# The opening of a sliding-window attention and feed-forward kernel, issued in another order

## Chip, cores, metric

One NeuronCore of one Trainium2 chip. The metric is the device time of one execution in microseconds (us); a median of several runs is given.

## What is computed

Attention over 8 batches, 8 heads, 576 positions and 64 features per head, in which a position sees only those at most 32 away, followed by a feed-forward pair with a leaky ReLU between:

```python
B, H, S, D = q.shape                       # 8, 8, 576, 64
scores = (q @ k.transpose(0, 1, 3, 2)) / sqrt(D)
scores = where(abs(pos[:, None] - pos[None, :]) <= 32, scores, -1e9)
attn = exp(scores - max(scores));  attn = attn / sum(attn)
x = (attn @ v).transpose(0, 2, 1, 3).reshape(B * S, H * D)      # 4608 x 512
h = x @ w_in                               # 512 x 2048
out = maximum(0.01 * h, h) @ w_out         # 2048 x 512, result 4608 x 512 f32
```

## The kernel before

The kernel's instructions go to each engine in the order in which the program writes them; nothing reorders them. So the order of the lines is the order of every engine's queue, and an engine whose next instruction waits holds all that is behind it.

The work is cut into units `i`: a unit is one batch, one half of the positions (288 queries) and one pair of heads. Eight units make a batch; units 0 to 3 are the first half of batch 0 for its four pairs, units 4 to 7 the second half. A unit goes through these steps:

- `score(i)` (L270): five matmuls on PE into the one score buffer `ps`, the exponential on ACT (L280, `e`), and the product with the band mask on POOL (L282, `prob`). The next unit's matmuls need the exponential to have read `ps`.
- `sums(i)` (L295): on PE the sum over keys of `prob`, by two matmuls with a block of ones into the one buffer `s` (L304), then the reciprocal on DVE (L309, `r`).
- `product(i)` (L312): five matmuls of `prob` with the values into the one buffer `x` (L320).
- `scaled(i)` (L332): `x` times `r` on DVE into `xT` (L334), the input of the feed-forward part; it frees `x`.

Ahead of a unit the queries, keys and values of its pair must be ready. `load_qk` and `load_v` load them in f32 by DMAs on SP's queue (`qf`, `kf`, `vf`). `cast_qk` (L186) casts to bf16: the queries on DVE or ACT, as its argument says, the keys on POOL. `transposes(0)` (L218) is a generator: each `next(first)` makes six PE transposes of a pair's queries, or then of its keys (L225), and their copy out of PSUM on ACT (L233, L239). `place_keys` (L248) copies transposed keys into the block-diagonal `kbd` on DVE, two copies a pair (L258). `cast_v` (L199) casts the two heads' values into the block-diagonal `vbd`, on POOL (L205) or ACT (L203). `make_mask` makes a half's band mask in two POOL copies (L163, L165).

`load_w_in` and `load_w_out` (L447, L450) load the weights, cast to bf16 on the way, in four DMAs each, issued on POOL's queue, where each issue takes its place among POOL's work. `keep_busy(t, lo, n)` (L398) is n matmuls without a use, in an unused part of `t`, that keep PE working (L402).

The feed-forward part goes by half batches: `h_first(0)` (L369) runs the first four tiles of h with the contraction outermost, so that each `next(h0)` needs one more pair's `xT`; `h_tile` (L360) then runs the others, 16 tiles for a half. From there on PE has dense work, into which the attention of later units is woven: `second_half()` (L525) inserts units 4 to 7 of batch 0 after chosen tiles, and from batch 1's second half on a plan with due times (L571 to L618) does so. `o_tile` (L382) is the second matrix product. The change touches only the opening, L461 to L505, up to the first `next(h0)`.

Of the kernel before, what the change touches and what calls it, by code (L numbers as in the profile page):

```python
# [16 lines left out]
def kernel(  # L17
# [14 lines left out]
    nc = tc.nc  # L32
# [128 lines left out]
    def make_mask(hf):  # L161
        lo = (16, 32)[hf]
        nc.gpsimd.tensor_copy(out=mask[hf][:, 0], in_=win_f[:, :, lo:lo + EVEN])  # L163
        lo = (16, 0)[hf]
        nc.gpsimd.tensor_copy(out=mask[hf][:, 1, :, lo:lo + 128], in_=win_f[:, :, 0:128])  # L165
# [4 lines left out]
    ps = scps.tile([128, 1024], FP32)  # L170
# [15 lines left out]
    def cast_qk(b, p, q_eng=None):  # L186
        for eng, src, dst in ((q_eng or nc.gpsimd, qf, qb), (nc.gpsimd, kf, kb)):
            if b < BY_DMA:
                parts = [(dst[:, p], src[b, p].rearrange("p a (c d) -> p c a d", d=D))]
            else:  # L190
                by_c = src[b, p].rearrange("p a (g c d) -> c p g a d", g=3, c=2)
                parts = [(dst[:, p, 3 * c:3 * c + 3], by_c[c]) for c in range(2)]
            for to, tok in parts:
                if eng is nc.scalar:
                    eng.activation(out=to, in_=tok, func=AF.Copy)
                else:
                    eng.tensor_copy(out=to, in_=tok)  # L197

    def cast_v(b, p, on_act=False):  # L199
        for a in range(2):  # L200
            r = slice(64 * a, 64 * a + 64)
            if on_act:
                nc.scalar.activation(out=vbd[b % 2][r, p, :, r], in_=vf[b, p][r], func=AF.Copy)  # L203
            else:
                nc.gpsimd.tensor_copy(out=vbd[b % 2][r, p, :, r], in_=vf[b, p][r])  # L205
# [42 lines left out]
    def place_keys():  # L248

        while landing and landing[0][0] <= state["done"]:  # L250
            unplaced.append(landing.pop(0)[1:])
        while unplaced:
            b, p, kT = unplaced.pop(0)
            for a in range(2):
                r = slice(64 * a, 64 * a + 64)
                to = kbd[b % 2][r, p, :, r]
                if b < BY_DMA:
                    nc.vector.tensor_copy(out=to, in_=kT[r].rearrange("p (n j) -> p n j", j=64))  # L258
                else:
                    nc.vector.tensor_copy(  # L260
                        out=to.rearrange("p n (m c) -> p n c m", c=2),
                        in_=kT[r].rearrange("p (c n m) -> p n c m", c=2, n=NB),
                    )
# [3 lines left out]
    def where(i):  # L267
        return i // 8, (i // 4) % 2, i % 4

    def score(i):  # L270
        b, hf, p = where(i)
        by_c = qT[b][:, p].rearrange("p (c i) -> p c i", c=2)
        for n_, blocks in enumerate(WIN[hf]):
            for blk, i0, n in blocks:
                nc.tensor.matmul(  # L275
                    ps_v[:, n_, :, i0:i0 + n], kbd[b % 2][:, p, blk],
                    by_c[:, :, hf * EVEN + i0:hf * EVEN + i0 + n], start=True, stop=True,
                )
        e = attn.tile([128, 2 * HALF], BF16, name="e")
        nc.scalar.activation(out=e, in_=ps[:, P0:P0 + 2 * HALF], func=AF.Exp, scale=scale)  # L280
        pr = prob[:, i % NPROB]
        nc.gpsimd.tensor_mul(  # L282
            pr.rearrange("p n c i -> p (n c i)"), e, mask[hf].rearrange("p n c i -> p (n c i)"),
        )
        probs[i] = [pr, None, None]
# [9 lines left out]
    def sums(i):  # L295

        b, hf, p = where(i)
        pr, both, _ = probs[i]
        s = xps.tile([128, HALF], FP32, name="s")
        if both is not None:  # L300
            nc.tensor.matmul(s, ones_bd, both, start=True, stop=True)  # L301
        else:
            for n in range(2):
                nc.tensor.matmul(  # L304
                    s, ones_bd, pr[:, n].rearrange("p c i -> p (c i)"),
                    start=(n == 0), stop=(n == 1),
                )
        r = recip.tile([128, HALF], FP32, name="r")
        nc.vector.reciprocal(r, s)  # L309
        probs[i][2] = r  # L310

    def product(i):  # L312

        b, hf, p = where(i)
        pr = probs[i][0]
        x = xps.tile([128, HALF], FP32, name="x")
        x_v = x.rearrange("p (c i) -> p c i", c=2)
        parts = [(n_, *block) for n_ in range(2) for block in WIN[hf][n_]]
        for n_, blk, i0, n in parts:
            nc.tensor.matmul(  # L320
                x_v[:, :, i0:i0 + n], vbd[b % 2][:, p, blk, :], pr[:, n_, :, i0:i0 + n],
                start=(blk == parts[0][1]), stop=(blk == parts[-1][1]), skip_group_check=True,
            )
        probs[i][1] = x

    def place(i):

        b, hf, p = where(i)
        t0 = (b * S + hf * HALF) % RING
        return xT[:, p, t0:t0 + HALF]  # L330

    def scaled(i):  # L332
        _, x, r = probs.pop(i)
        nc.vector.tensor_mul(place(i), x, r)  # L334
# [11 lines left out]
    def h_mms(g, f, h, cs):  # L346
        for c in cs:
            nc.tensor.matmul(  # L348
                h[:, 0:HALF], w_in_bf[:, c, ts(f, 128)], xT[:, c, ds(g * HALF % RING, HALF)],
                start=(c == 0), stop=(c == DMC - 1),  # L350
            )

    def h_out(g, f, h):

        nc.scalar.activation(  # L355
            out=gT[:, f, ds(g * HALF % RING, HALF)].rearrange("p (i c) -> p i c", c=2),
            in_=h[:, 0:HALF].rearrange("p (c i) -> p i c", c=2), func=AF.Prelu, alpha=0.01,
        )
# [10 lines left out]
    def h_first(g):  # L369

        hs = [mmps.tile([128, 512], FP32, name="mm", tag="mm") for _ in range(4)]
        yield hs[0]
        for c in range(DMC):
            for f in range(4):
                h_mms(g, f, hs[f], (c,))
            if c == DMC - 1:
                for f in range(4):
                    h_out(g, f, hs[f])
            yield
# [18 lines left out]
    def keep_busy(t, lo, n):  # L398


        for _ in range(n):
            nc.tensor.matmul(  # L402
                t[:, lo:lo + 224], ones_bd, mask[0].rearrange("p n c i -> p (n c i)")[:, 0:224], start=False, stop=False,
                skip_group_check=True,
            )
# [14 lines left out]
    def step():  # L420


        i = state["done"]
        if JOINED - 1 <= i < NC - 1:
            join(i + 1)
        if i < NC - 2:
            score(i + 2)
        weighted(i)
        place_keys()
        for b, p in qk_due.get(i, ()):  # L430
            cast_qk(b, p)
            transpose_dma(b, p)
            if 2 < b < B - 1:
                load_qk(b + 1, p)
        if 12 < i <= 12 + NPAIR:
            load_qk(3, i - 13)
        for b, p in v_due.get(i, ()):
            cast_v(b, p)
            if b + 1 < B:
                load_v(b + 1, p)  # L440
        state["done"] += 1
# [5 lines left out]
    def load_w_in(f0, f1):  # L447
        nc.gpsimd.dma_start(out=w_in_bf[:, :, f0:f1], in_=w_in_r[:, :, f0:f1])  # L448

    def load_w_out(i):  # L450
        c = slice(4 * i, 4 * i + 4)
        nc.gpsimd.dma_start(out=w_out_bf[:, c, :], in_=w_out_r[:, c, :])

    first = transposes(0)

    def first_pair():
        next(first)
        next(first)
        place_keys()
# [2 lines left out]
    make_mask(0)  # L462
    cast_qk(0, 1, nc.vector)
    first_pair()
    first_pair()
    cast_v(0, 0)
    score(0)
    cast_qk(0, 2, nc.vector)
    score(1)
    sums(0)  # L470
    next(first)
    next(first)
    product(0)
    keep_busy(ps, 0, 2)
    place_keys()
    cast_qk(0, 3, nc.scalar)
    load_w_in(0, 512)
    scaled(0)
    sums(1)
    keep_busy(ps, 0, 3)  # L480
    load_w_in(512, 1024)
    load_w_in(1024, 1536)
    next(first)
    score(2)
    next(first)
    cast_v(0, 1, on_act=True)
    load_w_in(1536, 2048)
    make_mask(1)
    place_keys()
    keep_busy(ps, 0, 8)  # L490
    sums(2)
    score(3)
    load_w_out(0)
    product(1)
    scaled(1)
    cast_v(0, 2, on_act=True)
    score(4)
    h0 = h_first(0)
    h = next(h0)
    keep_busy(h, HALF, 8)  # L500
    product(2)
    scaled(2)
    sums(3)
    cast_v(0, 3, on_act=True)
    load_w_out(1)  # L505

# [140 lines left out]
```

## Time and profile before

| | |
|---|---|
| median of 3 runs | 319.5 us (319.1 to 320.05) |
| profiled execution: span, first to last instruction | 318.5 us |
| around the span: median less span | 1.0 us |
| PE, DVE, ACT, POOL busy | 95%, 69%, 57%, 60% |
| TensorE clock granted | 1.000 from 19.15 us on |
| first dense matmul of h (third `next(h0)` complete) | 26.39 us |

Of the profiled execution the profile gives the span, and no other time of its own. A row of a group or of the timeline has a start in us from the span's start, a length, the engine, the line, the operation and the tiles it writes and reads (`out<-in`); "x5" is five instructions merged. PE stands for matmuls, PEld for weight loads. The chain is the sequence of work that ended last, followed backwards from the last instruction. The length of a matmul in a row is from its issue to its modelled end; the next can be issued well before that.

### The profile page before, as it was taken

The page shows a single profiled execution, that of the slowest core. Times are in us where ns is not written, and L with a number is a line of the kernel's source. Part 1 is how long each engine was busy: PE and PEld are TensorE (multiplying, and loading weights), DVE is VectorE, ACT ScalarE, POOL GpSimd, SP SyncE. Part 2 cuts the span into 40 slices and gives each one's busy share as a digit, 9 for nine tenths or more (in the row PEclk, how much of TensorE's full clock was granted, in tenths as well). Part 3 has the DMA queues.
Part 4 walks back from the last instruction along what each step waited for, and adds up shares of the span by engine and source line. Part 5 has one row for each costly group of instructions (what it writes and reads, how often), then busy time and mean ns, then how long its engine had stood idle before and what let it go on. Part 6 is the DMA issues. An engine that isn't in the chain of part 4 may idle for free.

```text
span 318.5 us, 6474 instructions
## 1 busy us (share of the span) xinstructions
PE 303.2 (95%) x2449; PEld 204.3 (64%) x2449; DVE 218.2 (69%) x259; ACT 182.6 (57%) x393; POOL 191.6 (60%) x251
## 2 busy tenths in 40 slices
PE   2679998999999999999999999999999999999996
PEld 1467774585765858576765858576665858576653
DVE  5678955869655997688755997688745988565100
ACT  7577698474652828374652828375552837464531
POOL 7798963974546866686546866586637866330000
PEclk9999999999999999999999999999999999999999
DMA  8999999997999995399735995399733430000101
GB/s 179 211 186 218 267 250 203 250 206 181 216 242 196 231 206 150 82 251 203 155 76 127 238 227 136 75 223 232 162 76 104 109 70 33 35 35 2 66 31 71
DMA packets 108400, 49.46 MB, mean 155 GB/s; under 512 B 68816, under 2 KB 103888, under 8 KB 108368
## 3 DMA queue, kind: packets, MB, share of 16 engines
q1 hardware_dynamic: 104144, 44.84, 66.8%
q0 software_dynamic: 4224, 4.19, 8.0%
q8 instruction: 19, 0.31, 0.4%
q14 instruction: 13, 0.11, 0.1%
HBM read 36.70 MB, written 9.44 MB: 145 GB/s over the span
## 4 chain that ended last, share of the span: by engine, by line
PE 89%; DMA 3%; DVE 2%; SPq 1%; POOL 1%; ACT 1%; issue 1%; DVEq 0%; ACTq 0%
PE mm L348 39%; PE mm L390 38%; PE x L320 5%; PE ps L275 4%; DMA kf<-in_k_dram 3%; PE s L301 2%; DVE r L309 2%; SPq L79 1%; POOL w_in_bf L448 1%; DVE xT L334 1%; PE tp L225 1%; PE s L304 1%; ACT vbd L203 0%; SPq L91 0%; POOL prob L282 0%
## 5 line engine op out<-in xcount | busy, mean ns | idle before, releaser
L309 DVE RECIPROCAL r<-s 128x288 f32<-128x288 f32 x64 | 125.2, 1956 | 56.5 <-PE s L301 53.3
L282 POOL TENSOR_TENSOR prob<-e,mask 128x576 bf16<-128x576 bf16 x64 | 81.5, 1274 | 87.8 <-ACT e L280 41.1
L348 PE MATMUL mm<-xT,w_in_bf 128*128 128x288 bf16 x1024 | 134.0, 286 | 0.3
L390 PE MATMUL mm<-w_out_bf,gT 128*128 128x512 bf16 (+2 forms) x592 | 130.4, 373 | 0.2 <-DMA w_out_bf<-in_moe_w_out_dram 0.2
L355 ACT ACTIVATE gT<-mm 128x288 bf16<-128x288 f32 x256 | 101.4, 412 | 24.8 <-PE mm L348 8.5
L348 PEld LDWEIGHTS <-w_in_bf 128*128 128x128 bf16 x1024 | 98.4, 98 | 24.8 <-issue 0.6
L390 PEld LDWEIGHTS <-gT 128*128 128x128 bf16 x592 | 56.3, 98 | 59.6 <-issue 0.3
L395 ACT ACTIVATE o_sb<-mm 128x512 f32<-128x512 f32 (+2 forms) x37 | 21.7, 586 | 92.0 <-PE mm L390 92.0
L280 ACT ACTIVATE e<-ps 128x576 bf16<-128x576 f32 x64 | 41.4, 648 | 9.4 <-PE ps L275 9.2
L197 POOL CAST kb<-kf 96x384 bf16<-96x384 f32 (+1 forms) x56 | 35.5, 656 | 4.6 <-DMA kf<-in_k_dram 4.6
L205 POOL CAST vbd<-vf 64x576 bf16<-64x576 f32 x50 | 34.5, 689 | 1.8 <-DMA vf<-in_v_dram 0.4
L334 DVE TENSOR_TENSOR xT<-x,r 128x288 bf16<-128x288 f32 x64 | 29.3, 458 | 8.2 <-PE x L320 1.2
L260 DVE COPY kbd<-kT 64x576 bf16<-64x576 bf16 x48 | 32.3, 672 | 0.3
L275 PE MATMUL ps<-qT,kbd 128*128 128x128 bf16 (+2 forms) x320 | 26.5, 215 | 1.8 <-DVE kbd L258 1.2
L275 PEld LDWEIGHTS <-kbd 128*128 128x128 bf16 x320 | 21.0, 100 | 10.6 <-DVE kbd L258 1.5
L320 PE MATMUL x<-prob,vbd 128*128 128x128 bf16 (+2 forms) x320 | 26.0, 213 | 1.3 <-ACT vbd L203 0.7
L197 POOL CAST qb<-qf 96x384 bf16<-96x384 f32 x48 | 24.5, 538 | 0.0
L320 PEld LDWEIGHTS <-vbd 128*128 128x128 bf16 x320 | 20.6, 99 | 3.9 <-ACT vbd L203 1.8
L292 DVE TENSOR_TENSOR both<-prob 128x288 bf16<-128x288 bf16 x52 | 19.7, 380 | 0.9
L301 PE MATMUL s<-both,ones_bd 128*128 128x288 bf16 x52 | 14.9, 286 | 0.0
L258 DVE COPY kbd<-kT 64x576 bf16<-64x576 bf16 x16 | 7.1, 444 | 8.7 <-ACT kT L239 8.6
L225 PE MATMUL tp<-ident,qb 96*128 96x96 bf16 x48 | 4.4, 243 | 6.2 <-DVE qb L197 6.2
(43 smaller groups left out, 86.6 us busy)
## 6 DMA issues: line engine op xcount, KB each, us to landing
qf<-in_q_dram SPq DMA_DIRECT2D x32, 288.0 KB, 4.5
kf<-in_k_dram SPq DMA_DIRECT2D x32, 288.0 KB, 5.0
vf<-in_v_dram SPq DMA_DIRECT2D x64, 144.0 KB, 4.2
out_dram<-o_sb SPq DMA_DIRECT2D x35, 256.0 KB, 3.6
w_in_bf<-in_moe_w_in_dram POOLq DMA_DIRECT2D x4, 512.0 KB, 8.6
w_out_bf<-in_moe_w_out_dram POOLq DMA_DIRECT2D x4, 512.0 KB, 16.8
qT<-qb SPq DMA_TRANSPOSE x24, 4.1
kT<-kb SPq DMA_TRANSPOSE x24, 3.2
```

What stands on the lines that cost most here:

```text
L197: eng.tensor_copy(out=to, in_=tok)
L205: nc.gpsimd.tensor_copy(out=vbd[b % 2][r, p, :, r], in_=vf[b, p][r])
L260: nc.vector.tensor_copy(out=to.rearrange("p n (m c) -> p n c m", c=2), in_=kT[r].rearrange("p (c n m) -> p n c m", c=2, n=NB),)
L275: nc.tensor.matmul(ps_v[:, n_, :, i0:i0 + n], kbd[b % 2][:, p, blk], by_c[:, :, hf * EVEN + i0:hf * EVEN + i0 + n], start=True, stop=True,)
L280: nc.scalar.activation(out=e, in_=ps[:, P0:P0 + 2 * HALF], func=AF.Exp, scale=scale)
L282: nc.gpsimd.tensor_mul(pr.rearrange("p n c i -> p (n c i)"), e, mask[hf].rearrange("p n c i -> p (n c i)"),)
L309: nc.vector.reciprocal(r, s)
L320: nc.tensor.matmul(x_v[:, :, i0:i0 + n], vbd[b % 2][:, p, blk, :], pr[:, n_, :, i0:i0 + n], start=(blk == parts[0][1]), stop=(blk == parts ...
L334: nc.vector.tensor_mul(place(i), x, r)
L348: nc.tensor.matmul(h[:, 0:HALF], w_in_bf[:, c, ts(f, 128)], xT[:, c, ds(g * HALF % RING, HALF)], start=(c == 0), stop=(c == DMC - 1),)
L355: nc.scalar.activation(out=gT[:, f, ds(g * HALF % RING, HALF)].rearrange("p (i c) -> p i c", c=2), in_=h[:, 0:HALF].rearrange("p (c i) -> ...
L390: nc.tensor.matmul(o[:, lo:hi], gT[:, f, ds(128 * j % RING, 128)], w_out_bf[:, f, lo:hi], start=(f == 0), stop=(f == FFC - 1),)
```

## The change

`cast_v` gets an argument that says which of the two heads to cast. In the opening, the first pair's scores are issued ahead of the second pair's key transposes, with the second half of the first value cast behind them; sums 0 (and so reciprocal 0) ahead of the cast of queries 2, which goes from DVE to ACT; score 2 ahead of query transposes 3; the weight DMAs one or two at a time between POOL's casts and mask products, in place of three ahead of the third mask product; the second mask behind the fourth mask product; and sums 3 (with its reciprocal) ahead of `scaled(2)`.

```diff
-    def cast_v(b, p, on_act=False):
-        for a in range(2):
+    def cast_v(b, p, on_act=False, heads=range(2)):
+        for a in heads:
             r = slice(64 * a, 64 * a + 64)
...
     make_mask(0)
     cast_qk(0, 1, nc.vector)
     first_pair()
-    first_pair()
-    cast_v(0, 0)
+    next(first)
+    cast_v(0, 0, heads=(0,))
     score(0)
-    cast_qk(0, 2, nc.vector)
+    cast_v(0, 0, heads=(1,))
+    next(first)
+    place_keys()
+    sums(0)
+    cast_qk(0, 2, nc.scalar)
     score(1)
-    sums(0)
+    product(0)
     next(first)
     next(first)
-    product(0)
+    scaled(0)
+    place_keys()
     keep_busy(ps, 0, 2)
-    place_keys()
-    cast_qk(0, 3, nc.scalar)
     load_w_in(0, 512)
-    scaled(0)
     sums(1)
     keep_busy(ps, 0, 3)
+    cast_qk(0, 3, nc.scalar)
     load_w_in(512, 1024)
-    load_w_in(1024, 1536)
-    next(first)
     score(2)
     next(first)
+    next(first)
+    keep_busy(ps, 0, 8)
     cast_v(0, 1, on_act=True)
+    load_w_in(1024, 1536)
     load_w_in(1536, 2048)
-    make_mask(1)
     place_keys()
-    keep_busy(ps, 0, 8)
     sums(2)
     score(3)
-    load_w_out(0)
+    make_mask(1)
     product(1)
     scaled(1)
     cast_v(0, 2, on_act=True)
     score(4)
+    load_w_out(0)
     h0 = h_first(0)
     h = next(h0)
     keep_busy(h, HALF, 8)
     product(2)
+    sums(3)
     scaled(2)
-    sums(3)
     cast_v(0, 3, on_act=True)
     load_w_out(1)
```

## The prediction

> **What bounds the kernel now.** I read the page first, then the chain that ended last from 0 to 45 us, then the timeline of the opening, the windows and PE's waits. The page:
>
> ```profile
> span 318.5 us, 6474 instructions
> PE 303.2 (95%) x2449; PEld 204.3 (64%) x2449; DVE 218.2 (69%) x259; ACT 182.6 (57%) x393; POOL 191.6 (60%) x251
> ```
>
> PE is the bound. The windows (length, then each engine's busy time and count) show where it isn't:
>
> ```profile
> 19.15:22.57 3.42, 2.49 (x31) 2.01 (x28) 2.74 (x4) 2.73 (x5) 3.39 (x5) 1.00 1.24 206
> 25.98:29.40 3.42, 3.28 (x36) 2.63 (x35) 3.08 (x4) 2.69 (x8) 2.56 (x3) 1.00 1.24 202
> 61.00:318.50 257.50, 254.40 (x2002) 169.51 (x2000) 174.32 (x205) 136.59 (x309) 143.49 (x190) 1.00 0.66 140
> ```
>
> From 26.39 on PE stops four times, for 1.20 us in all: 0.13 at 37.46, 0.22 at 48.84 (w_out), 0.71 at 51.06 (vbd), 0.14 at 60.47. The order there isn't touched. The stops at 51.06 and 60.47 follow from PE's own transposes and sums, and the wait for w_out lies in front of the 0.71, which would take it up. So the span moves by as much as the dense stream starts sooner or later, and the chain of the opening says what starts it (start, length, what):
>
> ```profile
> 15.54 0.82 POOL kb L197
> 16.36 2.35 POOL w_in_bf L448 x3
> 18.72 0.01 issue
> 18.73 1.30 POOL prob L282
> 20.03 0.04 issue
> 20.07 0.42 PE s L304 x2
> 20.49 0.03 issue
> 20.52 1.97 DVE r L309
> 22.49 0.02 issue
> 22.51 0.47 DVE xT L334
> ...
> 23.02 0.41 PE x L320 x5
> 23.43 0.02 issue
> 23.45 0.46 DVE xT L334
> 23.91 1.88 DVE r L309
> ...
> 26.39 0.65 PE mm L348 x4
> ```
>
> Three weight issues on POOL stand before the third mask product, then DVE's reciprocals follow one another: 3.92 us from the end of reciprocal 2 (22.48) to 26.39. The clock of PE shows in the timeline's keep_busy rows, 3 in 0.77 us and later 8 in 0.93:
>
> ```profile
> 15.92 0.77 PE L402 MATMUL ps<-mask,ones_bd 128*128 128x224 bf16 x3
> 21.75 0.93 PE L402 MATMUL mm<-mask,ones_bd 128*128 128x224 bf16 x8
> ```
>
> That is 0.187 us apiece before and 0.096 after; the trace has full clock granted from 19.15.
>
> **The change, walked queue by queue.** Durations are the trace's: six transposes 0.66 (the next PE group may start after 0.48), PSUM copy 0.65, kbd pair 0.91, score or product 0.65 at half clock and 0.40 at full, sums 0.64 and 0.41, exp 0.65, mask product 1.27, reciprocal 1.95, scaled 0.46, hand-over 0.04 to 0.09. The same walk over the old order meets the trace within 0.2 us at each step.
>
> First scores. kbd 0 is ready at 8.69, but PE stands behind the key transposes until POOL's cast at 9.37. Now score 0 runs at 8.75, exp at 9.44, mask product 0 at 10.18 to 11.45 (was 11.46 to 12.73). Key transposes 1 still start at 9.43; their copy on ACT lands behind exp 0 at 10.12, where it was: no cost. The second half of the value cast slips to 11.41 to 12.08 on POOL, which is idle until kf 2 lands at 12.68, so it is hidden with 0.6 us; product 0, its only reader, starts at 12.4.
>
> Sums 0 at 11.51 (was 12.78), reciprocal 0 at 12.2 (was 13.45). Score 1 now waits behind sums 0: 11.95 (was 11.77). ACT's cast of q 2 (0.83, row of q 3) at 11.45 holds nothing. Both are hidden by mask product 1, which stands behind POOL's cast k 2, whose data land at 12.68 in either order. That cast took 1.09 beside DVE's f32 cast of 1.39, and 0.82 (k 3) beside other DVE work; DVE now does a reciprocal there, so I take 0.82 and keep 1.09 as the other end. It gives 13.55, key copy 2 at 14.31, kbd 2 at 15.00 to 15.91 (was 16.18).
>
> Weights. POOL's order was product 1, k 3, w_in x3, product 2; now product 1 (to 14.80), w_in 0 (0.93, to 15.69), k 3 to 16.47 (0.10 later), w_in 1 to 17.2, product 2. Score 2 no longer stands behind query transposes 3: 15.96 (was 16.97), exp 2 16.66 to 17.31 (was 17.75), mask product 2 17.40 to 18.67 (was 18.73 to 20.02). The eight keep_busy wait for exp 2 and take PE from 17.37 to 18.87, so sums 2 starts at 18.87 (was 20.07), and reciprocal 2 at 19.46: 1.06 us earlier.
>
> SP's queue keeps its order. w_in 0 issued 1.55 us earlier meets the last value loads; vf 3 landed at 19.05 and 19.74 and is read at 22.6 and 23.3, and product 3 needs it at 25.1. The first packets of w_in came 2.4 us after its issue, so now at 17.15, with under 0.3 MB of values to go. By the trace's packets values move at 181 GB/s alone (17 us) and at 74 where they share with weights (46 us): 4.0 us, and 1.3 from last packet to landing, so 22.5 at the latest. That is hidden, with 0.8 us in hand on ACT. w_in 2 (18.6, 0.67 later) and w_out 0 (24.0, 1.3 later) queue behind weights that landed only at 24.39 and 30.83: nothing. Without that cover w_out 3 (48.80) would be late by up to 1.3, less the 0.7 of the stop at 51.06.
>
> Reading the second half on: key copy 3 ends 18.53, kbd 3 19.47, score 3 19.53, exp 3 20.62, value casts 2 on ACT end 21.95 (was 22.88), scaled 1 ends 21.91, product 2 starts at 22.01 (was 23.02). make_mask(1) moves behind mask product 3 (ends 21.98); mask product 4 runs at 22.8 to 24.1 (was 23.70): 0.9 earlier, and nobody is late.
>
> Reciprocal 3 ahead of scaled 2. Sums 3 ends at 22.66; reciprocal 3 22.70 to 24.65 (was 25.78); scaled 2 only now, 24.57 to 25.03 (was 23.91). Queued behind it are product 3, which needs x free, and the third group of h, which needs this xT. Product 3 25.08 (was 25.02), h c=2 25.32, scaled 3 25.52 to 25.98 (was 26.34), sums 4 25.81 (was 25.83), reciprocal 4 26.26 to 28.21 (was 26.29 to 28.25), h c=3 26.06 (was 26.39). Sums 5 waits for reciprocal 4: 28.26 (was 28.39).
>
> So 1.06 comes in at reciprocal 2 and 1.03 goes back, since the way from reciprocal 2's end to reciprocal 4's start grows from 3.81 (22.48 to 26.29) to 4.84 (21.42 to 26.26). Sums 5 gains another 0.1, because PE itself reached it 0.14 after reciprocal 4 and now stands waiting for it. The sum is -0.1 us against the profiled span of 318.5. The median of the runs, 319.5, lies 1.0 above that span (launch and end, untouched): **319.4 us**. With k 2 at 1.09 the walk gives +0.2; with the walk's own 0.2 to 0.3 of error either way, -0.4 to +0.4, 319.1 to 319.9. A measurement of this kernel tells 0.3%, 0.96 us, from no change; this is well inside.
>
> A rule that speaks against it: in the trace k 3's cast took 0.82 us beside DVE's kbd copies (15.33 to 16.18), no more than k 1 at 8.55, so those copies don't hold POOL. The Trainium skill, "DMA: Bandwidth & Descriptors", section "SWDGE vs HWDGE vs iDMA", says that GpSimd writes DMA descriptors to SBUF and that DVE locks it out in its two-port modes. By it w_in 0 (14.76 to 15.69) would wait out the copies of kbd 2, k 3 and product 2 would slip, by my estimate reciprocal 2 by 0.3, and the sum would be +0.2. I hold to the row.
>
> **The rivals.**
> *The early gain stays (faster).* If PE is given full clock before 19.15, or the reciprocal's order binds less than I say, the 1.06 us reach the stream. For: mask product 2 really comes 1.3 us earlier. Against: reciprocal 3 takes 1.95 whatever its place, and scaled 2 stands behind it. Full clock 3 us sooner makes the eight keep_busy and sums 2 shorter but moves mask product 2 not at all: 0.2 to 0.3. The whole gain would give 318.4.
>
> *The early gain fails to come (slightly slower).* The longer DVE chain is then paid alone: +0.9, 320.4, if reciprocal 2 starts at 20.5 as before; it decides at 19.6, where I break even. Likeliest cause: full clock comes only after 22.5, with the second eight keep_busy at 0.187 (1.5 us for 0.77) ahead of product 2; the walk has +0.7 then.
>
> *PE loses its clock (slower).* PE now idles from 23.9 to 25.1, 1.2 us in one piece, where the longest stop after 19.15 was 0.56. At half clock each 2 us lose 1. From dense work at 12.78 to the release it took 6.4 us, so up to 3.2; I price half, +1.6: 321.1. Against: in 19.15 to 22.57 PE was busy for 2.49 of 3.42 us and kept its clock; the new 22.57 to 25.98 has about 2.2. It decides if those 0.3 us matter. The Trainium skill, "TensorE: Matmul & The Clock Gate", section "HAM oscillation — how this bites in real kernels", wants over 3.4 us of idleness for that; by it this case falls away.
>
> **How the numbers follow.** Forecast (no change) 0.55; early gain stays 0.2, three quarters of it beyond 0.3%; gain fails 0.15, half of it beyond; clock lost 0.1, all beyond. That is faster 0.15 and slower 0.18; a walk through so many queues may be off on either side by more than I allow, so 0.18, 0.58, 0.24. Range: down to the whole gain, 318.4, and up past the failed gain to 320.6; its top leaves out the lost clock.
>
> **What would show it.** Right: score 0 at 8.75, mask product 2 at 17.4, reciprocal 2 near 19.5, scaled 2 after reciprocal 3 near 25.0, PE idle before product 3, reciprocal 4 again near 26.3, sums 5 within 0.4 of 28.4. Wrong: mask product 2 after 18, a keep_busy at 0.187 after 21 or any matmul at double length after 25, a stop over 1 us at 40 to 52, or scaled 2 before reciprocal 3.

## The result, and the profile after

The changed kernel took 320.07 us (median of 6 runs, 320.05 to 320.78); the kernel before, beside it, 319.3 us (6 runs, 318.96 to 320.05). The ratio is 1.0032, 95% interval 1.0017 to 1.0046: slower, by 0.77 us in the medians. Measured again beside 29 runs of before (median 319.58) it was 320.08 us, ratio 1.0025 (1.0015 to 1.0035), 0.50 us in the medians; the recorded ratios aren't simply quotients of the medians. One of the 12 executions of that repeat took 1806 us and is left out of the ratio.

The page of the changed kernel, and its window of the stage in which the dense stream starts (length, then busy time and count by engine):

```profile
span 319.0 us, 6455 instructions
PE 301.1 (94%) x2429; PEld 203.5 (64%) x2449; DVE 220.7 (69%) x258; ACT 183.5 (58%) x394; POOL 191.2 (60%) x251
```

```profile
22.57:25.98 3.41, 2.17 (x25) 1.72 (x23) 2.58 (x3) 1.81 (x3) 3.41 (x5) 1.00 1.23 202
```

PE is busy for 2.17 us there; the 2.2 were forecast, and its clock stayed. The chain that ended last shows why it waits (start, length, what):

```profile
22.42 1.96 DVE r L309
24.38 0.32 DVE xT L334
24.70 0.14 issue
24.84 0.40 PE x L320 x5
25.23 0.49 PE mm L348 x4
25.73 0.26 PE s L304 x2
26.01 1.97 DVE r L309
27.98 0.05 issue
28.02 0.42 PE s L304 x2
```

Reciprocal 3 stands ahead of the scaled product 2; product 3, h c=2, sums 4 and reciprocal 4 follow one another behind it. Before, the scaled product stood first and the last group of h (c=3) came out of the chain at 26.39. Even so sums 5 starts at 28.02, 0.37 us sooner than the 28.39 of before. The span is 0.5 us longer all the same, and a second place, at 42 to 45 us, shows a stop that before didn't have. The timeline there (start, length, engine):

```profile
41.79 0.82 POOL L197 CAST kb<-kf 96x768 bf16<-96x768 f32 x1 [2.19 <-DMA kf<-in_k_dram]
...
41.80 3.21 DVE L197 CAST qb<-qf 96x768 bf16<-96x768 f32 x1
...
42.55 2.05 POOL L567 MEMSET vbd<- 128x1152 bf16 x2
...
45.07 0.43 PE L225 MATMUL tp<-ident,qb 96*128 96x96 bf16 x6 [0.66 <-DVE qb L197]
```

POOL's cast begins 15 ns ahead of DVE's. DVE's, 0.56 us long in the profile of before, where it began 0.07 us ahead of POOL's, ends at 45.01, after POOL's memsets, and PE stops for 0.66 us. So there were two suspects for the slowdown: the order of reciprocal 3 and the scaled product (the prediction's own term, which should have been paid for), and the meeting of the two casts.

### The profile page after: what moved, and what is told of

The parts are those of the page before. It is cut to its first block, busy times and chain, and to the rows that moved or that the text cites. A ratio compares the mean times of both kernels' runs of the same rounds, so it can differ in the third digit from the quotient of the medians.

```text
span 319.0 us, 6455 instructions
## 1 busy us (share of the span) xinstructions
PE 301.1 (94%) x2429; PEld 203.5 (64%) x2449; DVE 220.7 (69%) x258; ACT 183.5 (58%) x394; POOL 191.2 (60%) x251
## 4 chain that ended last, share of the span: by engine, by line
PE 88%; DVE 5%; ACT 3%; issue 2%; POOL 1%; ACTq 0%; POOLq 0%; DVEq 0%
PE mm L390 38%; PE mm L348 37%; PE x L320 5%; PE ps L275 5%; PE s L301 2%; DVE r L309 2%; DVE qb L197 1%; PE s L304 1%; DVE kbd L258 1%; POOL prob L282 1%; ACT kT L239 1%; PE tp L225 1%; ACT e L280 1%; ACT vbd L203 1%; DVE kbd L134 1%
## 5 line engine op out<-in xcount | busy, mean ns | idle before, releaser
L390 PE MATMUL mm<-w_out_bf,gT 128*128 128x512 bf16 (+2 forms) x572 | 128.7, 373 | 1.1
L197 POOL CAST kb<-kf 96x384 bf16<-96x384 f32 (+1 forms) x56 | 34.8, 643 | 4.5 <-DMA kf<-in_k_dram 4.3
```

What stands on the lines that cost most here:

```text
L390: nc.tensor.matmul(o[:, lo:hi], gT[:, f, ds(128 * j % RING, 128)], w_out_bf[:, f, lo:hi], start=(f == 0), stop=(f == FFC - 1),)
```

## The experiments

**Both kernels again, nothing altered.** The changed kernel:

> The changed kernel again, nothing altered, to see which stops repeat. Port theory: in the profile of the changed kernel DVE's cast of queries 2 of batch 1 (start 41.80, 3.21 us, where before had 42.15 and 0.56 us) began 15 ns after POOL's key cast and was held until POOL's two memsets had ended; PE stopped 0.66 us for it at 45.07. It should do so again in this profile: cast over 3 us, a stop of about 0.6 us near 45, and the time about 0.8 us above before. Order theory (reciprocal 3 ahead of the scaled product 2 costs the time): reciprocal 4 starts near 26.3 or later and sums 5 at 28.4 or later, against 28.39 before. If both are wrong, the difference is in the chance of the run (clock released at 15.5 or 19.2 us, loads landing up to 1 us apart) and this run is level with before.

The kernel before:

> The kernel before again, nothing altered, for a second profile. Port theory: DVE's cast of queries 2 of batch 1 starts ahead of POOL's key cast (by 0.07 us in the first profile) and takes about 0.6 us, no stop near 45; if in this run it starts behind, it takes over 2 us and the span is about 0.8 us longer. Order theory: sums 5 at 28.4 or, with an earlier clock, up to 1 us sooner. Span 317.4 to 318.5.

The changed kernel: 320.08 us, its profiled execution 320.12 us with a span of 318.4. DVE's cast began at 42.05, ahead of POOL's (42.16), took 0.56 us, and there was no stop near 45. So the meeting isn't what makes the usual execution long. Sums 5 started at 28.28. The kernel before: 319.13 us, span 317.4, a full 1.1 us less than its first profile. Its POOL and DVE rows of the third mask product, and then those of the changed kernel:

```profile
14.15 0.81 POOL L197 CAST kb<-kf 96x768 bf16<-96x768 f32 x1
...
14.91 2.41 POOL L448 DMA_DIRECT2D w_in_bf<-in_moe_w_in_dram  x3
...
17.62 1.27 POOL L282 TENSOR_TENSOR prob<-e,mask 128x576 bf16<-128x576 bf16 x1 [0.30 <-ACT e L280]
...
19.39 1.96 DVE L309 RECIPROCAL r<-s 128x288 f32<-128x288 f32 x1 [0.36 <-PE s L304]
```

```profile
14.71 0.93 POOL L448 DMA_DIRECT2D w_in_bf<-in_moe_w_in_dram  x1
...
15.63 0.83 POOL L197 CAST kb<-kf 96x768 bf16<-96x768 f32 x1
...
17.35 1.27 POOL L282 TENSOR_TENSOR prob<-e,mask 128x576 bf16<-128x576 bf16 x1 [0.20 <-ACT e L280]
...
19.32 1.96 DVE L309 RECIPROCAL r<-s 128x288 f32<-128x288 f32 x1
```

In this execution of before the loads landed sooner, keys 1 at 7.63 and not at 8.49, keys 3 at 13.54 and not at 15.49. The cast of keys 3 started at 14.15 and reciprocal 2 at 19.39, where the first profile had 20.52. The changed kernel's cast of keys 3 stands behind a weight issue and starts at 15.60 to 15.71 in the six profiles with that issue in front and keys 3 landing at 13.96 to 15.32; in this one reciprocal 2 starts at 19.32. The early gain is 0.07 us here.

**The cast of queries 2 moved away from POOL's.** `cast_qk` gets an argument that picks queries (0) and keys (1).

```diff
     def second_pair(p):
+        if p == 0:
+            cast_qk(1, 2, nc.vector, (0,))
         next(second)
...
-            cast_qk(1, p + 2, nc.vector)
+            cast_qk(1, p + 2, nc.vector, (1,) if p == 0 else (0, 1))
```

> The changed kernel with the cast of queries 2 of batch 1 on DVE issued ahead of the pair's key copies, so that it runs at about 40 us while POOL is idle (39.6 to 41.8) and can't meet POOL's key cast. Port theory: the cast takes 0.56 us, the stop of 0.66 us near 45 goes, and the time falls by 0.6 to 0.9 us, to 0 to 0.4 us below before. Order theory and chance of the run: nothing changes, still 0.8 us above before, since the cast was not what set the time.

320.07 us, ratio to before 1.0012 (1.0003 to 1.0021). The cast ran at 40.25 for 0.56 us, as meant, and of 12 executions none was over 320.28. In the changed kernel 4 of 18 stood at 320.7 to 320.8; the one of them that was profiled is the one with the 3.21 us cast. The median didn't move, so the theory of the casts falls as the cause of the usual difference. For the minority it holds as far as one profile of the four and their absence here show it: 0.6 to 0.7 us each.

**The scaled product 2 ahead of sums 3 again, all else as changed.**

```diff
     product(2)
-    sums(3)
     scaled(2)
+    sums(3)
```

> The changed kernel with one part undone: the scaled product 2 ahead of sums 3 and its reciprocal, as before. Prediction's sum: reciprocal 3 starts about 0.7 us later and the scaled product 2 ends 1.1 us sooner, so that sums 5 starts 0.5 to 1.0 us sooner, near 27.3. Order theory: the time falls by 0.5 to 1.0 us. Port theory: PE's early gain is lost again at the cast near 42 to 45, since the key data land when they land and POOL's cast then stands ahead of DVE's or behind it: the time falls by less than 0.3 us if the cast is still held, by up to 1 us if PE's sooner start lets DVE's cast begin ahead of POOL's.

319.15 us against the changed kernel's 320.08 on the same chip: 0.93 us less, and below before, ratio 0.9987 (0.9978 to 0.9995). Sums 5 started at 27.92 in this profile, not near 27.3, because of an effect that the prediction had called hidden:

```profile
15.17 8.79 DMA vf<-in_v_dram
...
23.99 0.69 ACT vbd L203
...
24.72 0.41 PE x L320 x5
```

The last half of the values of pair 3 landed at 23.96. The weights had begun at 17 us, in an execution with late loads, and from 18 to 23.6 us the values and other loads of SP's queue moved 0.15 MB beside 1.01 MB of weights. That execution took 319.75 us, the longest of the 12; the repeat's profile, with the last half at 18.32, didn't have it.

> The changed kernel with the scaled product 2 ahead of sums 3, as before, once more: a second time, and a profile of one of its shorter runs. Order theory: median about 0.9 us below the changed kernel, 0.3 to 0.5 us below before; in the profile PE's stop before product 3 is under 0.3 us when the values of pair 3 land by 20 us, reciprocal 4 starts at 25.0 to 25.3. Rival (the first measurement was chance): level with before.

319.08 us, ratio 0.9977 (0.9965 to 0.9990). The chain of this profile, with the scaled product where it was before:

```profile
22.50 0.46 DVE xT L334
22.95 1.88 DVE r L309
...
24.92 0.47 DVE xT L334
...
25.43 0.65 PE mm L348 x4
```

The last group of h (c=3) comes at 25.43 with reciprocal 4 at 25.33, and sums 5 at 27.59; the changed kernel had reciprocal 4 at 26.01 and 26.26 with reciprocal 2 at nearly the same place (19.07 and 19.32 against 19.39).

**That part of the change alone.**

```diff
     product(2)
+    sums(3)
     scaled(2)
-    sums(3)
```

> The kernel before with one part of the change alone: sums 3 and its reciprocal ahead of the scaled product 2. Order theory: the scaled product 2 ends 1.1 us or more later, product 3, h c=2, sums 4 and reciprocal 4 follow, and there is no early gain to pay for it: the time rises by 0.8 to 1.1 us, to about 320.5; PE stops for 1.0 to 1.3 us before product 3. Rival (PE's later work has slack that takes this up, and what the changed kernel loses is lost in its first 20 us): less than 0.3 us.

320.48 us against 319.49 beside it: 0.99 us more, ratio 1.0029 (1.0017 to 1.0041). PE stopped for 1.23 us before product 3, as in the changed kernel (1.24). The price of the order is confirmed from both sides, 0.93 and 0.99 us. The profiles have it free of the landings: from the start of reciprocal 2 to the start of reciprocal 4 the opening of before takes 5.77 us in each of the four profiles with its own order, and 6.77 with the exchange; the changed kernel takes 6.94 (both profiles) and, with the scaled product back, 5.94 in the four profiles whose values came in time. The exchange is 1.00 us of this way both times, and 0.17 us of the changed kernel's longer way is there without it.

**Keys 3 landing later, in both kernels.**

```diff
     load_qk(0, 2)
+    load_v(0, 1)
     load_qk(0, 3)
-    for p in range(1, NPAIR):
+    for p in range(2, NPAIR):
```

> The kernel before with the values of pair 1 loaded ahead of queries and keys 3, so that keys 3 land about 1.5 us later (13.5 to 15.5 us in the profiles so far) and nothing else changes. Landing theory (before, the cast of keys 3 with the three weight issues and mask product 2 behind it on POOL starts when the keys land, so its opening is as late as its data): reciprocal 2 moves from 19.4 by 1.0 to 1.5 us and the time rises by about 1 us, to 320.6. Rival (the runs of before differ for the clock's release or something else, not for the landing): under 0.3 us.

> The changed kernel with the same later landing of keys 3. Landing theory: the cast of keys 3 stands behind a weight issue until 15.6 anyway, so that of 1.5 us at most 0.5 is felt: reciprocal 2 at 19.1 to 19.6, the time level with the changed kernel's 320.1 to within 0.4, and so level with or below the kernel before when that is delayed in the same way. Rival: both kernels lose the same.

Before: 320.73 us (7 runs, three of them at 322.4 to 323.6, which nothing here explains), ratio 1.0062 (1.0034 to 1.0090), 1.2 us more. Changed: 320.15 us, ratio to the unaltered before 1.0027 (1.0012 to 1.0042), 0.1 us more than without the delay. The timelines of POOL, of before and of the changed kernel so delayed:

```profile
16.05 0.82 POOL L198 CAST kb<-kf 96x768 bf16<-96x768 f32 x1 [1.36 <-DMA kf<-in_k_dram]
16.82 2.41 POOL L449 DMA_DIRECT2D w_in_bf<-in_moe_w_in_dram  x3
```

```profile
16.27 0.81 POOL L198 CAST kb<-kf 96x768 bf16<-96x768 f32 x1 [0.68 <-DMA kf<-in_k_dram]
```

In before the keys landed at 16.00, three weight issues follow and reciprocal 2 starts at 21.02, though this execution had full clock from 16.21; in the changed kernel they landed at 16.21 and it starts at 19.58. So a late landing of keys 3 is paid by the opening of before and hardly by the changed one, and the early clock didn't make up for it.

Whether it was keys 3 in the undelayed executions, their profiles tell. POOL's cast of keys 1, PE's score 0 and POOL's mask product 0 in the first profile of before, in its second, and in the first of the changed kernel:

```profile
8.55 0.82 POOL L197 CAST kb<-kf 96x768 bf16<-96x768 f32 x1 [1.49 <-DMA kf<-in_k_dram]
...
9.89 0.65 PE L275 MATMUL ps<-qT,kbd 128*128 128x96 bf16 x5
...
11.46 1.27 POOL L282 TENSOR_TENSOR prob<-e,mask 128x576 bf16<-128x576 bf16 x1 [0.44 <-ACT e L280]
```

```profile
7.69 0.82 POOL L197 CAST kb<-kf 96x768 bf16<-96x768 f32 x1 [0.31 <-DMA kf<-in_k_dram]
...
9.03 0.65 PE L275 MATMUL ps<-qT,kbd 128*128 128x96 bf16 x5
...
10.60 1.27 POOL L282 TENSOR_TENSOR prob<-e,mask 128x576 bf16<-128x576 bf16 x1 [0.61 <-POOL vbd L205]
```

```profile
8.29 0.82 POOL L197 CAST kb<-kf 96x768 bf16<-96x768 f32 x1 [1.23 <-DMA kf<-in_k_dram]
...
8.75 0.64 PE L275 MATMUL ps<-qT,kbd 128*128 128x96 bf16 x5 [0.56 <-DVE kbd L258]
...
10.28 1.27 POOL L282 TENSOR_TENSOR prob<-e,mask 128x576 bf16<-128x576 bf16 x1 [0.56 <-DMA vf<-in_v_dram]
```

In before POOL waits for keys 1, score 0 stands behind their transposes, and mask product 0 starts 2.91 us after the cast of keys 1 in all five profiles with that opening. In three of them (keys 1 landing at 7.63, 7.86, 8.11) reciprocal 2 follows 11.7 us after that cast, at 19.39, 19.62 and 19.86, though full clock came at 16.46, 18.69 and 18.62; POOL cast keys 3 there straight behind mask product 1, without waiting for their landing (13.54, 14.31, 14.43). Only in the first profile did it wait for keys 3, for 0.49 us: of the 1.13 us between the first two profiles of before, keys 1 make 0.86 and keys 3 the other 0.27. In the changed kernel and its versions score 0 no longer stands behind those transposes: mask product 0 starts at 10.27 to 10.38 in all nine profiles, with keys 1 landing at 7.78 to 8.68, and reciprocal 2 at 19.07 to 19.39 in the eight undelayed. No run delays keys 1 alone, so their part is read from the profiles and not tested by an edit.

**The meeting of the casts, forced in the kernel before.** `idle_f` is a tile of 128x384 f32 that nothing reads.

```diff
+        if p == 0:
+            nc.vector.memset(idle_f, 0.0)
         if p + 2 < NPAIR:
             cast_qk(1, p + 2, nc.vector)
```

> The kernel before with one added DVE memset of 128x384 f32 (0.35 us by the rate of the kbd memset, 1.98 us for 2304) ahead of the cast of queries 2 of batch 1, so that the cast starts behind POOL's key cast in every run. Port theory: the cast then takes over 2 us, PE stops for 0.4 to 0.9 us near 45 and the time rises by 0.5 to 0.8 us. Rival (the cast's length doesn't matter, other work has slack for it): the time stays within 0.2 us.

320.39 us against 319.49, ratio 1.0030 (1.0013 to 1.0046). The timeline:

```profile
41.40 0.82 POOL L198 CAST kb<-kf 96x768 bf16<-96x768 f32 x1 [2.13 <-DMA kf<-in_k_dram]
...
41.78 2.84 DVE L198 CAST qb<-qf 96x768 bf16<-96x768 f32 x1
...
44.68 0.43 PE L226 MATMUL tp<-ident,qb 96*128 96x96 bf16 x6 [0.81 <-DVE qb L198]
```

An added 0.38 us on DVE costs 0.9, by a stop of 0.81 us. The mechanism is real; it decides single executions of the changed kernel, not its median.

**Three versions of the shorter kernel.** To the version with the scaled product back in its place, the later first weight issue, the earlier cast, or both, were added.

```diff
-    load_w_in(0, 512)
     sums(1)
     keep_busy(ps, 0, 3)
     cast_qk(0, 3, nc.scalar)
+    load_w_in(0, 512)
     load_w_in(512, 1024)
```

> The same with the first weight issue moved behind the cast of keys 3 on POOL, so that the weights start about 1 us later. Overtaking theory (in the first profile of this version the last half of the values of pair 3 landed at 23.96, 4.7 us later than in the changed kernel, because the weights had started while values were still to go, and PE stopped for 1.06 us): no run with a late landing is left, the longer runs go, the median falls by 0 to 0.2 us. Rival (the first weights then come too late for h): they land at about 22, PE stops at h c=0 by up to 0.3 us and the median rises.

> The version with the scaled product 2 ahead of sums 3, and the cast of queries 2 of batch 1 ahead of the key copies. Port theory: the runs in which POOL's key cast gets ahead of DVE's cast (0.6 us longer) go; they were 4 of 18 in the changed kernel, so the median moves little and the highest run falls. Rival: no difference to the version without it.

> All three together. If both theories hold: 318.9 to 319.1 us with runs within 0.4 us of each other, 0.4 to 0.6 us below before. If the first weights come too late: 0.2 us above the version without that part.

On one chip, beside before at 319.60 us: with later weights 319.46 us, 1.0000 (0.9984 to 1.0016), with runs from 318.91 to 321.34; with the earlier cast 319.16, 0.9983 (0.9972 to 0.9994); with both 319.15, 0.9987 (0.9974 to 0.9999). None is told from the plain version (0.9977). The later weights did not take the longer executions away: the values landed by 18.49 in its profile, but that execution stopped for 0.75 us at 64.75, a place none of the edits touches. What those later stops come from stays open.

The version that beats both kernels is the change without its last exchange: 319.08 and 319.15 us in two measurements.

## Why the prediction was wrong

**The walk of the new order was right.** Forecast against the two profiles of the changed kernel: mask product 2 at 17.40 (17.13, 17.35), reciprocal 2 at 19.46 (19.07, 19.32), reciprocal 3 at 22.70 (22.42, 22.67), product 3 at 25.08 (24.84, 25.09), reciprocal 4 at 26.26 (26.01, 26.26), sums 5 at 28.26 (28.02, 28.28). The span was to be 318.4; the second profile and most executions have 318.4. Queries 2 on ACT gave the key cast its 0.82 us, the end taken. The first weight issue took 0.93 us beside the key copies, as long as in before (16.31 to 17.24), where it stood beside none of them, so holding to the row against the rule was right. The price of reciprocal 3 ahead of the scaled product, 1.03, measured 0.93 and 0.99 in time and 1.00 in the profiles.

**The step that failed** is the one that set this span beside the median: "The median of the runs, 319.5, lies 1.0 above that span (launch and end, untouched)". Every execution whose span is recorded took 1.65 to 1.78 us more than its span. By that, a span of 318.5 is an execution of about 320.2; the profiled one was among the longest of its kernel, whose 92 recorded spans have a median of 317.9 and go from 316.9 to 319.4. With 1.7 in place of 1.0 the forecast span gives 320.1, and 320.07 was measured. So "no change" compared a walk that starts from a long execution with a median of usual ones, and the change came out slower by 0.32%, with an interval of 0.15% on either side.

**The same error in the sum** is the term of 1.06 us at reciprocal 2. It was worked out against an execution in which keys 1 landed at 8.49 and keys 3 at 15.49, both the latest of the undelayed profiles with the opening of before. Against the other three (reciprocal 2 at 19.39 to 19.86) the changed kernel's 19.07 to 19.39 is a gain of 0 to 0.8. The versions with the scaled product in its place are 0.43 and 0.52 us below before in the median, so about 0.5 us came in and 0.9 went out. The warning stood in my own lines: "PE stands behind the key transposes until POOL's cast at 9.37" takes the length of a wait for keys 1 from one execution, and "k 3 to 16.47 (0.10 later)" compares a start set by a queue with one set by a landing. The new order takes the dependence on these landings away, so it gains only where they were late. It also makes the time steadier: most executions of the changed kernel lie at 320.0 to 320.1, those of before are spread from 318.6 to 321.1.

**The rivals.** "The early gain fails to come" was nearest, with 320.4 for a gain of nothing; but its cause was not the clock, which came at 15.5 and 17.4 in the changed kernel. The gain was small because the loads of before usually land sooner than in the first profile. "PE loses its clock" did not happen with a stop of 1.24 us and 2.17 us of work in the window. The clock's release at 15.52 moved reciprocal 2 by at most 0.3, as the first rival had it.

**Two covers were thinner than said.** Values 3 were to land by 22.5 at the latest; in one execution, of the version with the scaled product back, they landed at 23.96. (The first packet of the weights in the first profile starts at 18.02, 1.7 us after the issue and not the 2.4 that I read; in the changed kernel it starts at 16.97 and 17.30, close to the 17.15 of the forecast.) And "the order there isn't touched" is no proof that the span follows the dense stream: PE's timetable moved against the DMAs', and the casts at 42 us changed places in a few executions.

## What to carry to other kernels

One profile is one execution: set its own time in the spread of the runs before any span is turned into a time, and where its chain of waits begins with a landing, work the sum for an early and a late landing. A reordering that takes a wait on data away gains only in the executions in which the data were late; what it pays in queue order it pays in all. Ahead of a single buffer, the operation that frees the buffer goes first: here a 2 us reciprocal in front of a 0.46 us product cost 0.9 to 1.0 us, because everything behind that buffer waited.

## What the runs showed of the hardware

A DVE cast of f32 from SBUF, 0.56 us alone, took 3.21 and 2.84 us when POOL's cast of 0.82 us had begun before it and two POOL memsets followed without a gap; it ended 0.4 us after the last of them. The Trainium skill, "SBUF — State Buffer", section "Who interferes with whom", has DVE and GpSimd share a port pair as an exclusive lock that the first one keeps for its whole instruction. These runs agree on who waits, and add that the wait ran on over three POOL instructions in a row.

The same loads at the start landed up to 2 us apart from one execution to the next (keys 3 at 13.54 to 15.49 us, keys 1 at 7.63 to 8.68, with the loads in the order of before), and full clock was granted anywhere from 15.3 to 19.2 us.
